# Late row blocks as three rounded products in a Fourier-filter and GEGLU kernel: splits queued behind named operations, and the first pair's place in the third tile

## The chip, the core and the metric

The kernel runs on one core of one Trainium2 chip. The metric is the device time of one execution in microseconds (us); less is better. Engines are named as in the profile: PE does matrix products (PEld is its loading of weights), ACT, DVE and POOL work element by element, and SP's queue issues the DMAs.

## What is computed

The reference is a two-part layer on a sequence of 2048 rows with 512 features. The first part is a filter in the frequency domain with a residual, the second a gated feed-forward layer with a residual:

```python
x = A_x                                           # (1, 2048, 512)
X = rfft2(layernorm(x)); X = X * (w_r + 1j * w_i)
h = x + irfft2(X)
g = layernorm(h) @ w_gate; u = layernorm(h) @ w_up     # 512 -> 1376
h2 = h + (gelu(g) * u) @ w_down                        # 1376 -> 512
```

All inputs and outputs are fp32.

## The kernel before, in words

The rows are kept as 16 blocks of 128 (`NB` = 16); `gh[:, b]` in SBUF is block b, 128 partitions by 512 features. The filter is done as dense products with tables. Its last step for a block is the inverse transform over rows, one product of the 128x128 table `mis[:, b]` with the block's unfolded spectrum `gh[:, b]`, then a DVE operation that adds x, subtracts the mean and writes h back into `gh[:, b]`, and DVE statistics for the second layernorm.

The feed-forward layer works on half of the blocks at a time (q = 0: blocks 0 to 7, q = 1: blocks 8 to 15), and within a half on 11 tiles of 128 hidden units; 22 tiles in all, counted by n. A tile is seven groups of products, P0 to P6 (a Strassen-like scheme), each of six matmuls of 128x128 by 128x512, since each fp32 product is made from three rounded ones: a value is split into a rounded high part (ACT, type fp32r) and a low part (what is left, by a subtraction on DVE or POOL), and high by high, high by low and low by high are added up (`mm3`, L96 to L103; its three matmuls are at L100, L101 and L102).

`gate_up(n)` (L694) is a generator that records a tile in seven steps: P0 and copy c1; P1 and the addition d1; P2 and c2; P3; P4, c3 and dy; P5 with the first half's gelu, product m0 and split i0, o0; P6 with d2 and the second half's m1, i1, o1. The copies are at L651 (ACT), the additions d1, d2, dy at L654 (DVE), gelu at L657 (ACT), m at L660 (DVE), i at L666 (ACT, high part), o at L673 (DVE, low part). The products go to banks 0 to 2 of PSUM for even n, 3 to 5 for odd n. `down` (L732) records the products with w_down (L747) of a group of two or three finished tiles, one block of rows at a time, into bank 6 or 7 in turn (`bank_67`), each followed by a DVE addition into `gh` (L753, or L750 with the output's DMA). `fill(2)` records two such blocks.

Weights for a later tile come by `load_gu` (L127): two DMAs, four POOL operations (L138 to L146), one rounding copy of 128x1792 on DVE (L153, CAST), and three POOL subtractions for the low parts (L156: one of 128x256, two of 128x768). The rounded copy goes to one of two buffers, so it waits for the products of the tile two before. The helper `behind` (L116) gives as the reason of one such wait that it "leaves the shared port" to a DVE instruction. w_down comes by `load_d` (L489: a DMA, ACT L494, POOL L496).

While the first half's tiles run, the second half's blocks are finished off beside them: blocks 8, 12 and 9 were unfolded already, the others are unfolded by four POOL operations of 128x256 each (L809 to L812) when `late(b)` (L946) is first advanced; the second advance records the DMA of x (L954), the product (L956, one fp32 matmul, which the profile shows as two MATMUL records), the residual (L957, DVE) and the statistics (L505, L507). Blocks 8 and 12 have their products in tile 2, blocks 9 and 13 in tile 3, 10 in tile 4, 14 in tile 5, 11 in tile 6, 15 in tile 7. The py of such a block lies in bank 6 or 7, in the same turn as the `down` blocks.

What sets the order: up to the start of tile 2 a list written by hand (`FIRST`) fixes the order of PE, ACT, DVE and POOL. In the loop from n = 2 (L978) only PE's order is as recorded; a scheduler that simulates the engines places ACT's, DVE's and POOL's instructions when it builds the program, and each engine then runs its instructions in that fixed order, each waiting for its semaphores. `tc.issue_after(i)` keeps an instruction behind i in that placing. `reuse_waits` and the buffer counts of the pools (`w3`: two buffers unless said otherwise) set when a buffer comes free.

In the loop, one turn n advances the tile n: P1, then P2, then the second advance of the waiting `late` blocks, `fill(2)`, P3, `fill(2)`, P4, `fill(2)`, P0 of the tile n+1, `fill(2)`, the first advance of the next `late` blocks, P5, P6.

Of the kernel before, what the change touches and what calls it, by code (L numbers as in the profile page):

```python
# [12 lines left out]
F32 = mybir.dt.float32  # L13
F32R = mybir.dt.float32r
I32 = mybir.dt.int32
AF = mybir.ActivationFunctionType
ALU = mybir.AluOpType
PSUM = bass.MemoryType.PSUM

S, D, F = 2048, 512, 1376  # L20
P = 128
# [36 lines left out]
def kernel(  # L58
# [15 lines left out]
    nc = tc.nc  # L74
    pe, act, dve, pool = nc.tensor, nc.scalar, nc.vector, nc.gpsimd
# [423 lines left out]
    def row():  # L499
        return rp.tile([P, D], F32, name="row")  # L500
# [141 lines left out]
    def tile_of(n, i=slice(0, 4)):  # L642

        at = slice(i.start * P, i.stop * P)
        (x, y, z), by_pe = products(n, i)
        if n not in sums:
            sums[n] = sum_tiles()
        s1, u2, u3 = (t[:, at] for t in sums[n])

        def copy(to, a):  # L650
            return lambda: act.activation(to, a, AF.Copy)  # L651

        def add(to, a, b):
            return lambda: dve.tensor_tensor(to, a, b, op=ALU.add)  # L654

        def gelu(g):
            return lambda: act.activation(g, g, AF.Gelu_apprx_tanh)  # L657

        def times(u, g):
            return lambda: dve.tensor_tensor(u, u, g, op=ALU.mult)  # L660

        def high(k, u):
            def do():
                if n not in parts_of:
                    parts_of[n] = w3.tile([P, 2, 2, 512], F32R, name="a", bufs=3)
                act.activation(parts_of[n][:, 0, k, at], u, AF.Copy)  # L666

            return do

        def low(k, u):  # L670
            def do():
                a = parts_of[n][:, :, k, at]
                dve.tensor_tensor(a[:, 1], u, a[:, 0].bitcast(F32), op=ALU.subtract)  # L673

            return do

        return by_pe | {
            "c1": copy(s1, x),
            "d1": add(s1, y, s1),
            "c2": copy(u2, x),  # L680
            "c3": copy(u3, x),
            "dy": add(y, z, u3),
            "G0": gelu(s1),
            "m0": times(x, s1),
            "i0": high(0, x),
            "o0": low(0, x),
            "d2": add(u2, z, u2),
            "G1": gelu(u2),
            "m1": times(y, u2),
            "i1": high(1, y),  # L690
            "o1": low(1, y),
        }

    def gate_up(n):  # L694

        do = products(n)[1] if n == 2 else tile_of(n)

        def all_of(names):
            for k in names.split():
                ins = do[k]()  # L700
            return ins

        all_of("P0")
        if n == 2:

            yield
            do = tile_of(n)
            all_of("c1 P1 d1")
        else:
            all_of("c1")  # L710
            yield
            all_of("P1 d1")
        yield
        for names in ("P2 c2", "P3"):
            all_of(names)
            yield
        last = copied[n] = all_of("P4 c3")
        all_of("dy")
        yield

        for _ in load_d(tiles[n][1], last):
            pass

        for names in ("P5", "P6 d2"):
            all_of(names)
            k = names[1] == "6"
            with tc.issue_after(last.ins):
                do[f"G{k:d}"]()
            all_of(f"m{k:d} i{k:d} o{k:d}")
            yield  # L730
# [38 lines left out]
    orders = [list(range(NF)), [NF - 2, NF - 1, *range(NF - 3, -1, -1)]]  # L769
    tiles = [(q, f) for q, order in enumerate(orders) for f in order]  # L770
    downs = iter(())
    begun_tiles, wds, parts_of, hns, copied, sums = {}, {}, {}, {}, {}, {}
    bank_67 = itertools.cycle((6, 7))

    def sum_tiles():
# [11 lines left out]
    do = {}  # L787
# [140 lines left out]
    def step(n):  # L928

        if n not in begun_tiles:  # L930
            f = tiles[n][1]
            if f not in gu:
                for _ in load_gu(f):
                    pass
            begun_tiles[n] = gate_up(n)
        next(begun_tiles[n])
# [3 lines left out]
    with tc.manual_schedule(engines={et.PE, et.Activation, et.DVE, et.Pool}):  # L940
        for op in FIRST.split():
            name, *place = op.split(".")
            do[name](*map(int, place))


    def late(b):  # L946

        if b not in BY_THEN:

            with held("lo"):  # L950
                unfolded(b, row())
        yield
        xt = row()
        nc.sync.dma_start(xt, x3[:, b])  # L954
        py = ps[:, next(bank_67)]
        pe.matmul(py, mis[:, b], gh[:, b], start=True, stop=True)  # L956
        dve.scalar_tensor_tensor(gh[:, b], xt, mv[:, b, 0:1], py, op0=ALU.subtract, op1=ALU.add)  # L957
        for _ in stats2(b):
            pass
        yield  # L960
# [7 lines left out]
    def fill(n):  # L968
        for _ in range(n):
            next(downs, None)  # L970
# [7 lines left out]
    with tc.manual_schedule(engines={et.PE}):  # L978
        for n, (q, f) in list(enumerate(tiles))[2:]:
            k, at_change = n - q * NF, n == NF - 1  # L980
            if k == 0:
                step(n)
            step(n)
            if k > 8 and not q:
                for i in range(2 * k - 18, 2 * k - 16):
                    with tc.issue_after(copied[n - 1].ins):
                        hns[i] = [normed(b) for b in (8 + i, 12 + i)]
            step(n)
            if at_change:

                steps = [in_turn(i, hns[i], banks) for i, banks in enumerate(((3, 4), (5, 0), (3, 4), (1, 2)))]
                next(steps[0])
            for g in ending:
                next(g)
            if n in (6, 7):

                norm_scales(2 * n - 4, 2)
            fill(2)
            step(n)
            fill(2)  # L1000
            step(n)
            fill(2)

            if k == NF - 1:
                downs = down(q, orders[q][-3:], True)
            if at_change:
                next(steps[0])
                next(steps[1])
            elif k < NF - 1:
                step(n + 1)  # L1010
                fill(2)
            else:
                fill(1)
            ending = [late(b) for b in lates.get(n, ())]
            for g in ending:
                next(g)
            step(n)
            step(n)
            if k in (4, 7):
                downs = down(q, orders[q][: k + 1][-3:], False)  # L1020
            elif k == 1:
                downs = down(q, orders[q][:2], False)
            if at_change:
                gu = {f: gu[f] for f in orders[0][-2:]}
                for s in steps:
                    for _ in s:
                        pass
                    fill(2)
            if k == NF - 1:
                fill(12)  # L1030
# [125 lines left out]
```

## Time and profile before

| what | value |
| --- | --- |
| time, median of 3 runs | 455.23 us (455.15 to 455.26) |
| the profiled execution's own time | 455.09 us |
| its span (first to last instruction) | 453.3 us |
| PE busy / PEld / DVE / ACT / POOL | 438.1 / 371.2 / 276.7 / 206.5 / 276.0 us |
| granted PE clock, mean over the span | 0.998 |
| DMA moved | 41.05 MB, mean 91 GB/s |
| part of the span this change touches (tile 2's P2 to tile 7's late product) | 131.8 to 214 us |

In the rows of the trace's timeline the columns are: start and length in us, engine, line of the kernel, operation, the tiles it writes and reads, shapes, count, and in brackets the idle time before it with what ended it. Successive instructions of one engine overlap by some 0.04 to 0.17 us in these records, so the distance from start to start is the cost of one in a dense row. A row with a count of 2 or more covers several instructions merged. In the groups by line, the numbers after the bar are the busy time in us and the mean ns of one.

### The profile page before, as it was taken

Reading aid. Unit: us, or ns where it says so; the run is one execution under the profiler, and the core shown is the slowest. Engines: PE = TensorE matmul, PEld = TensorE weight load, DVE = VectorE, ACT = ScalarE, POOL = GpSimd, SP = SyncE. Lnnn points to the kernel's source line nnn. Section 1 sums busy time; section 2 is a strip of 40 time slices with the busy share of each in tenths; the row PEclk is TensorE's granted clock in tenths of the full one; section 3 lists DMA queues with packets and bytes.
Section 4 is the critical chain, followed back from the end, with each engine's and each line's share of the span. In section 5 each row is a group of like instructions: output and inputs, shape, how many; then the busy total and the mean of one; then the engine's idle time right before and its main releaser. Section 6 shows DMA issues by size and latency. Waiting matters only on the chain.

```text
span 453.3 us, 6435 instructions
## 1 busy us (share of the span) xinstructions
PE 438.1 (97%) x2289; PEld 371.2 (82%) x2289; DVE 276.7 (61%) x513; ACT 206.5 (46%) x433; POOL 276.0 (61%) x305
## 2 busy tenths in 40 slices
PE   3999999999999999999999999999999999999996
PEld 3999998788878777877888888888888888888875
DVE  5957886797565766358734579266655355635453
ACT  4979776688741243034322775242243024303420
POOL 6985996968869578738662643165566546663210
PEclk9999999999999999999999999999999999999999
DMA  8994805200032022112210213121122102210013
GB/s 293 392 395 145 274 11 185 95 25 1 25 116 74 31 83 93 48 46 71 69 46 25 70 40 123 48 93 46 26 69 71 46 24 71 69 46 25 23 70 117
DMA packets 21168, 41.05 MB, mean 91 GB/s; under 512 B 2064, under 2 KB 7696, under 8 KB 21008
## 3 DMA queue, kind: packets, MB, share of 16 engines
q1 hardware_dynamic: 20992, 40.51, 25.9%
q8 instruction: 18, 0.29, 0.3%
q10 hardware_dynamic: 144, 0.13, 0.1%
q14 instruction: 14, 0.11, 0.1%
HBM read 36.44 MB, written 4.19 MB: 90 GB/s over the span
## 4 chain that ended last, share of the span: by engine, by line
PE 93%; DVE 3%; ACT 2%; DMA 1%; issue 1%; SPq 0%; DVEq 0%
PE ps L747 26%; PE ps L100 15%; PE ps L102 15%; PE ps L101 15%; PE ps L288 5%; PE ps L416 3%; PE ps L515 3%; PE ps L427 3%; PE ps L448 2%; PE ps L848 1%; PE ps L956 1%; DMA gh<-in_x 1%; PE ps L554 1%; PE ps L548 1%; PE ps L845 0%
## 5 line engine op out<-in xcount | busy, mean ns | idle before, releaser
L100 PE MATMUL ps<-cb,gu 128*128 128x512 f32 (+1 forms) x336 | 127.8, 380 | 2.0 <-ACT s L651 1.6
L747 PE MATMUL ps<-wd,a 128*128 128x512 f32 (+1 forms) x537 | 125.9, 387 | 0.2 <-DVE gh L750 0.2
L102 PE MATMUL ps<-cb,gu 128*128 128x512 f32 (+1 forms) x336 | 124.8, 372 | 0.0
L101 PE MATMUL ps<-cb,gu 128*128 128x512 f32 (+1 forms) x336 | 124.8, 371 | 0.0
L747 PEld LDWEIGHTS ps<-wd,a 128*128 128x128 f32 x537 | 99.3, 188 | 22.0 <-DVE gh L957 1.0
L156 POOL TENSOR_TENSOR gu<-raw,gu 128x768 fp32r<-128x768 f32 (+1 forms) x54 | 78.3, 1479 | 39.8 <-DVE gu L153 36.0
L651 ACT ACTIVATE s<-ps 128x512 f32<-128x512 f32 (+1 forms) x72 | 40.4, 561 | 133.7 <-PE ps L102 133.4
L100 PEld LDWEIGHTS ps<-cb,gu 128*128 128x128 f32 x336 | 63.2, 188 | 14.9 <-ACT s L651 2.2
L101 PEld LDWEIGHTS ps<-cb,gu 128*128 128x128 f32 x336 | 63.3, 188 | 11.7 <-issue 1.0
L102 PEld LDWEIGHTS ps<-cb,gu 128*128 128x128 f32 x336 | 63.2, 188 | 11.0
L753 DVE TENSOR_TENSOR gh<-ps,gh 128x512 f32<-128x512 f32 x48 | 33.1, 691 | 53.4 <-PE ps L747 53.3
L496 POOL TENSOR_TENSOR wd<-wdr,wd 128x512 fp32r<-128x512 f32 x22 | 28.5, 1295 | 50.9 <-ACT wd L494 50.9
L660 DVE TENSOR_TENSOR ps<-ps,s 128x512 f32<-128x512 f32 (+1 forms) x48 | 31.0, 650 | 24.8 <-PE ps L102 22.5
L666 ACT ACTIVATE a<-ps 128x512 fp32r<-128x512 f32 (+1 forms) x48 | 26.9, 561 | 38.9 <-DVE ps L660 38.6
L138 POOL TENSOR_TENSOR raw<-raw 128x256 f32<-128x256 f32 x20 | 14.7, 737 | 38.3 <-DMA raw<-in_wgu 37.2
L673 DVE TENSOR_TENSOR a<-ps,a 128x512 fp32r<-128x512 f32 (+1 forms) x48 | 30.8, 641 | 11.5 <-ACT a L666 9.8
L654 DVE TENSOR_TENSOR s<-ps,s 128x512 f32<-128x512 f32 (+1 forms) x48 | 30.9, 643 | 10.3 <-PE ps L102 8.7
L657 ACT ACTIVATE s<-s 128x512 f32<-128x512 f32 (+1 forms) x48 | 28.2, 592 | 18.4 <-DVE s L654 18.4
L654 DVE TENSOR_TENSOR ps<-ps,s 128x512 f32<-128x512 f32 (+1 forms) x24 | 15.7, 654 | 27.7 <-ACT s L651 27.7
L288 PE MATMUL ps<-ms,pn 128*128 128x128 f32 x120 | 17.4, 295 | 7.6 <-ACT ms L256 7.4
L288 PEld LDWEIGHTS ps<-ms,pn 128*128 128x128 f32 x120 | 16.0, 209 | 8.0 <-POOL pn L263 7.4
L153 DVE CAST gu<-raw 128x1792 fp32r<-128x1792 f32 x18 | 19.6, 1091 | 4.5 <-PE ps L101 2.9
(124 smaller groups left out, 609.6 us busy)
## 6 DMA issues: line engine op xcount, KB each, us to landing
raw<-in_wgu SPq DMA_DIRECT2D x40, 256.0 KB, 3.1
wt<-in_w SPq DMA_DIRECT2D x16, 520.0 KB, 5.5
wdr<-in_wd SPq DMA_DIRECT2D x22, 256.0 KB, 2.7
out<-gh SPq DMA_DIRECT2D x15, 256.0 KB, 2.0
gh<-in_x SPq DMA_DIRECT2D x7, 512.0 KB, 8.0
row<-in_x SPq DMA_DIRECT2D x12, 256.0 KB, 3.0
mis<-in_mi SPq DMA_DIRECT2D x1, 1024.0 KB, 10.8
a<-in_x SPq DMA_DIRECT2D x4, 256.0 KB, 4.1
```

The source lines that it names most:

```text
L100: pe.matmul(o, lh, rh, start=(i == 0 and not onto), stop=False, skip_group_check=True)
L101: pe.matmul(o, lh, rl, start=False, stop=False, skip_group_check=True)
L102: last = pe.matmul(o, ll, rh, start=False, stop=(i == n - 1), skip_group_check=True)
L156: pooled["lo"] = pool.tensor_tensor(r[:, 1, m], t[:, m], r[:, 0, m].bitcast(F32), op=ALU.subtract)
L288: pe.matmul(pt[:, c], o, mc, start=(z == 0), stop=(z == len(parts[b][c]) - 1))
L496: pool.tensor_tensor(r[:, 1], t, r[:, 0].bitcast(F32), op=ALU.subtract)
L651: return lambda: act.activation(to, a, AF.Copy)
L654: return lambda: dve.tensor_tensor(to, a, b, op=ALU.add)
L660: return lambda: dve.tensor_tensor(u, u, g, op=ALU.mult)
L673: dve.tensor_tensor(a[:, 1], u, a[:, 0].bitcast(F32), op=ALU.subtract)
L747: pe.matmul(o, parts_of[tiles.index((q, f))][:, ha, i // 4, r], wds[f][:, hw, c], start=start, stop=stop)
L753: dve.tensor_tensor(gh[:, b, c], o, gh[:, b, c], op=ALU.add)
```

## The change

The single fp32 product of a late block becomes three rounded ones (`mm3`), for which both factors are split: two ACT copies (high parts of `gh[:, b]`, 128x512, and of `mis[:, b]`, 128x128) and two DVE subtractions (low parts), all from SBUF to SBUF. `late` gets a third stage: first advance unfolds, second splits, third does the product. The splits are kept behind two given operations: in tile 2 behind the last high and low part of the hand-written list (g1bi1, g1bo1), from tile 3 on behind the tile's c1 (ACT) and d1 (DVE). From tile 3 on the product stays behind P2; for the pair of tile 2 (blocks 8 and 12) it moves behind P4, past two `fill(2)`. The scratch for DMA descriptors is set to 4096 bytes, and two tiles `m` and `v` of two buffers each are new.

```diff
 def high(k, u):
-                act.activation(parts_of[n][:, 0, k, at], u, AF.Copy)
+                return act.activation(parts_of[n][:, 0, k, at], u, AF.Copy)
 def low(k, u):
-                dve.tensor_tensor(a[:, 1], u, a[:, 0].bitcast(F32), op=ALU.subtract)
+                return dve.tensor_tensor(a[:, 1], u, a[:, 0].bitcast(F32), op=ALU.subtract)
...
             do = tile_of(n)
-            all_of("c1 P1 d1")
+            begun[n] = do["c1"](), (do["P1"](), do["d1"]())[1]
         else:
-            all_of("c1")
+            c1 = do["c1"]()
             yield
-            all_of("P1 d1")
+            begun[n] = c1, (do["P1"](), do["d1"]())[1]
...
-            do[name](*map(int, place))
+            ins = do[name](*map(int, place))
+            if name == "g1bi1":
+                behind_act = ins
+            elif name == "g1bo1":
+                behind_dve = ins
...
     def late(b):
...
+        yield
+        m = w3.tile([P, 2, P], F32R, name="m")
+        v = w3.tile([P, 2, D], F32R, name="v")
+        for h, l, full in ((v[:, 0], v[:, 1], gh[:, b]), (m[:, 0], m[:, 1], mis[:, b])):
+            with tc.issue_after(behind_act.ins):
+                act.activation(h, full, AF.Copy)
+            with tc.issue_after(behind_dve.ins):
+                dve.tensor_tensor(l, full, h.bitcast(F32), op=ALU.subtract)
         yield
         xt = row()
         nc.sync.dma_start(xt, x3[:, b])
         py = ps[:, next(bank_67)]
-        pe.matmul(py, mis[:, b], gh[:, b], start=True, stop=True)
+        mm3(py, [((m[:, 0], m[:, 1]), (v[:, 0], v[:, 1]))])
...
             step(n)
+            if n > 2:
+                behind_act, behind_dve = begun[n]
+            for g in ending:
+                next(g)
...
             step(n)
-            for g in ending:
-                next(g)
+            if n > 2:
+                for g in ending:
+                    next(g)
...
             fill(2)
             step(n)
             fill(2)
             step(n)
+            if n == 2:
+                for g in ending:
+                    next(g)
             fill(2)
...
-    nc = bacc.Bacc("TRN2", target_bir_lowering=False, num_devices=1)
+    nc = bacc.Bacc("TRN2", target_bir_lowering=False, num_devices=1, dynamic_dma_scratch_size=4096)
```

In the diff of the loop, the four `step(n)` shown are P1, P2, P3 and P4 of the turn. `begun[n]` holds c1 and d1 of tile n.

In the built programs the change shows as follows. On DVE the new subtractions stand directly behind d1 of tiles 3 to 7, in the order v, m (v, m, v, m in tile 3), and m1 (L660), the residual (now L969) and o1 (L673) of the tile come behind them. In tiles 3 and 6 DVE's order ahead of them is CAST, d2, o0, d1, as before; in tile 4 the CAST moves from behind m1 to ahead of d1; in tiles 5 and 7 it stays behind m1. In tile 2 they stand behind the last o of the hand-written list, mixed with the first two `down` additions and ahead of the CAST. ACT's new copies stand behind c1, ahead of i0 or i1. On POOL one w_down subtraction (L496) moves ahead of two unfolding operations in tile 2. SP's order is the same.

More of the change, by code (lines that the diff above doesn't have):

```diff
@@ L771 @@
     downs = iter(())
-    begun_tiles, wds, parts_of, hns, copied, sums = {}, {}, {}, {}, {}, {}
+    begun_tiles, wds, parts_of, hns, copied, sums, begun = {}, {}, {}, {}, {}, {}, {}
     bank_67 = itertools.cycle((6, 7))
```

## The prediction

> **What bounds the kernel now.** I read the page first: busy time by engine, then the chain of work that ended last. Both say PE.
>
> ```profile
> PE 438.1 (97%) x2289; PEld 371.2 (82%) x2289; DVE 276.7 (61%) x513; ACT 206.5 (46%) x433; POOL 276.0 (61%) x305
> ...
> PE 93%; DVE 3%; ACT 2%; DMA 1%; issue 1%; SPq 0%; DVEq 0%
> ```
>
> Then the stage itself, by windows (length first, then busy time of PE, PEld, DVE, ACT and POOL):
>
> ```profile
> 131.77:142.01 10.24, 10.19 (x41) 7.35 (x40) 6.54 (x11) 0.60 (x1) 8.36 (x9) 1.00 0.14 47
> 154.26:165.54 11.28, 11.28 (x47) 8.64 (x46) 8.15 (x15) 4.53 (x8) 9.84 (x11) 1.00 0.29 93
> 213.14:453.30 240.16, 236.46 (x1064) 195.54 (x1062) 128.79 (x205) 84.25 (x156) 112.57 (x107) 1.00 0.17 57
> ```
>
> PE has no gap in the stage, and almost none in the 240 us behind it (236.46 of 240.16). So whatever PE loses or gains here arrives at the end in full, and PE only loses if something makes it wait. POOL works 9.84 of 11.28 us in the tile of the second row; that matters below.
>
> **The products.** PE's timeline, tile 3: 24 rounded products, then two fp32 products in four records.
>
> ```profile
> 148.81 0.39 PE L100 MATMUL ps<-cb,gu 128*128 128x512 f32 x1
> ...
> 154.03 0.39 PE L102 MATMUL ps<-cb,gu 128*128 128x512 f32 x1
> 154.26 1.88 PE L956 MATMUL ps<-gh,mis 128*128 128x512 f32 x4
> ```
>
> From 148.81 to 154.03 are 23 steps, 0.227 us each. The fp32 records end at 156.14 and the last rounded one at 154.42, so four records cost 1.72, or 0.86 a product. Three rounded ones cost 0.68. The gain is 0.18 a block, 1.4 us for eight blocks, if PE never waits. That is the whole prize, 0.3%.
>
> **What is added and can make PE wait.** Per block, two copies on ACT and two subtractions on DVE. ACT is idle where they stand, for instance 4.22 us ahead of i0 in tile 2's end:
>
> ```profile
> 151.18 0.60 ACT L666 ACTIVATE a<-ps 128x512 fp32r<-128x512 f32 x1 [4.22 <-DVE ps L660]
> ```
>
> Four copies of at most that row's 0.60 fit, so the high parts cost nothing. The subtractions are another matter: both inputs lie in SBUF, unlike the sums of the tiles, which read one from PSUM. The trace has few such DVE instructions; here are two places.
>
> ```profile
> 14.39 1.55 DVE L277 TENSOR_TENSOR uv<-pn 128x512 f32<-128x512 f32 x1
> 14.12 1.27 POOL L263 TENSOR_TENSOR pn<-gh 128x512 f32<-128x512 f32 x1
> 15.35 1.73 POOL L262 TENSOR_TENSOR pn<-gh 128x512 f32<-128x512 f32 x1
> 28.62 0.42 DVE L275 TENSOR_TENSOR us<-pn 128x256 f32<-128x256 f32 x1
> 73.04 1.87 POOL L94 TENSOR_TENSOR gu<-raw,gu 128x256 fp32r<-128x256 f32 x2
> 73.31 1.01 DVE L438 TENSOR_TENSOR z<-t,t 128x520 f32<-128x520 f32 x1
> 74.36 0.57 DVE L440 TENSOR_TENSOR z<-z 128x2 f32<-128x2 f32 x1
> ```
>
> L277 starts at 14.39 while POOL's L263 runs to 15.39, and ends at 15.94: it waited out the POOL instruction and then took 0.55. POOL's next one started at 15.35 and took 1.73 for 1.27: it waited meanwhile. The two exclude each other. The last three rows tell who is next when both want to go: POOL's second L94 stood waiting while L438 ran to 74.32; the tiny L440 came 0.04 later, and still took until 74.93, past the end of the L94 pair (74.91). So they alternate, one instruction each. With no POOL instruction in the way I take 0.60 from start to start for v (the step of the rows below) and 0.2 for m, estimated from 0.42 for 256 columns less 0.13 for each 128 (0.60 for 512 against 0.34 for 256); behind POOL 0.55 and 0.16.
>
> The Trainium skill (SBUF — State Buffer, Who interferes with whom) says the same: a DVE instruction with two SBUF inputs contends with a GpSimd instruction that reads SBUF, the loser being held for the whole instruction. By that rule the sum is the one below; without it, it is that of the third rival. The rows agree with it (1.55 for 0.55 at work).
>
> **Tile 3.** Call E the start of its P1 (151.53). P2 ends at E+2.73, and then PE wants v9's low part at E+2.96 (second product) and m9's at E+3.19.
>
> ```profile
> 151.56 1.09 DVE L153 CAST gu<-raw 128x1792 fp32r<-128x1792 f32 x1 [0.42 <-PE ps L101]
> 152.57 0.68 DVE L654 TENSOR_TENSOR s<-ps,s 128x512 f32<-128x512 f32 x1
> 153.17 0.68 DVE L673 TENSOR_TENSOR a<-ps,a 128x512 fp32r<-128x512 f32 x1
> 153.77 0.68 DVE L654 TENSOR_TENSOR s<-ps,s 128x512 f32<-128x512 f32 x1
> ...
> 152.74 4.34 POOL L156 TENSOR_TENSOR gu<-raw,gu 128x256 fp32r<-128x256 f32 x3 [4.48 <-DVE gu L153]
> 157.03 0.76 POOL L809 TENSOR_TENSOR row<-gh 128x256 f32<-128x256 f32 x1
> ...
> L156 POOL TENSOR_TENSOR gu<-raw,gu 128x768 fp32r<-128x768 f32 x36 | 65.8, 1849 | 0.0
> ```
>
> DVE is behind already: CAST, d2, o0, and d1 only at E+2.24. The subtractions stand behind d1, so v9 comes at E+2.84, where POOL is in the second of the three L156, which runs to E+3.75. Then, in turn: v9 to 4.30, third L156 to 6.10 (1.85 less the overlap of starts), m9 to 6.26, L809 (0.72 a step) to 6.98, v13 to 7.53, L810 to 8.25, m13 to 8.41. PE does what it can between; the last product waits for m13. A restart costs 0.17, by the rows of tile 2 below. End at 8.41 + 0.17 + 0.23 = E+8.81, before E+2.73+1.72 = E+4.45. **Tile 3: +4.4.** Behind these on DVE wait m1, the residuals and o1; they take some 2.5 us, to about E+11; PE asks for them at P1 of tile 4 (o1's bank), five groups of six (6.8 us) after E+8.8, so they cost nothing.
>
> **Tiles 4 and 6.** In tile 4 the CAST moves ahead of d1:
>
> ```profile
> 162.82 0.39 PE L100 MATMUL ps<-cb,gu 128*128 128x512 f32 x1
> 163.63 0.68 DVE L673 TENSOR_TENSOR a<-ps,a 128x512 fp32r<-128x512 f32 x1
> 165.59 1.08 DVE L153 CAST gu<-raw 128x1792 fp32r<-128x1792 f32 x1
> 166.75 2.54 POOL L156 TENSOR_TENSOR gu<-raw,gu 128x256 fp32r<-128x256 f32 x2 [1.57 <-DVE gu L153]
> ...
> 200.02 1.09 DVE L153 CAST gu<-raw 128x1792 fp32r<-128x1792 f32 x1 [0.42 <-PE ps L101]
> 201.20 4.35 POOL L156 TENSOR_TENSOR gu<-raw,gu 128x256 fp32r<-128x256 f32 x3 [3.03 <-DVE gu L153]
> ```
>
> With E = 162.82, o0 is at E+0.81, so CAST E+1.42, d1 E+2.43, v10 E+3.03. L156 follows the CAST's start by 1.16: E+2.6, its short one to E+3.3. v10 to 3.87, long L156 to 5.70, m10 to 5.86, end E+6.26; before E+2.73+0.86 = E+3.59. **+2.7.** Tile 6 has tile 3's order (E = 199.99, CAST E+0.03, L156 E+1.21): m11 to E+6.26, end E+6.66. **+3.1.** The CAST of tile 4 also waits for POOL's chain; PE's delay in tile 3 gives that chain more time than the subtractions take from it, so I add nothing.
>
> **Tiles 5 and 7.** The CAST stays behind, and d1 comes at E+1.57 (E = 173.24), v at E+2.17:
>
> ```profile
> 174.81 0.69 DVE L654 TENSOR_TENSOR s<-ps,s 128x512 f32<-128x512 f32 x1
> 177.57 0.74 POOL L146 TENSOR_TENSOR raw<-raw 128x256 f32<-128x256 f32 x1
> ```
>
> Free of POOL, both are in time: gain 0.18. POOL's chain that ends with this L146 (E+5.1) comes some 3 us earlier against E, since PE is late, so one instruction may still be met: -0.2 to +0.9, I take **+0.5 for tile 5 and -0.2 for tile 7** (two tiles' delay ahead of it).
>
> **Tile 2.**
>
> ```profile
> 131.77 1.88 PE L956 MATMUL ps<-gh,mis 128*128 128x512 f32 x4
> 133.69 3.02 PE L747 MATMUL ps<-wd,a 128*128 128x512 f32 x12
> 136.55 0.39 PE L100 MATMUL ps<-cb,gu 128*128 128x512 f32 x1
> ...
> 137.91 2.90 PE L747 MATMUL ps<-wd,a 128*128 128x512 f32 x12
> 140.65 0.39 PE L100 MATMUL ps<-cb,gu 128*128 128x512 f32 x1
> ...
> 132.89 0.75 DVE L957 SCALAR_TENSOR_TENSOR gh<-row,mv,ps 128x512 f32<-128x512 f32 x1 [1.27 <-issue]
> 132.21 0.73 POOL L138 TENSOR_TENSOR raw<-raw 128x256 f32<-128x256 f32 x1 [3.61 <-DMA raw<-in_wgu]
> ```
>
> Before, twelve L747 waited for the residual to free bank 6: it ended at 133.64, they began at 133.69 and took 2.86 for 2.74; so a restart costs 0.05 + 0.12. The pair and these twelve took 4.78. Behind P4 the pair meets the same wait: three products end sooner (0.68), the residual starts 0.26 later (132.89 against 131.77 + 0.86) and takes 0.75, so twelve begin at +1.75 for 1.36 of products, a wait of 0.5 for 0.33 before. The pair itself gains 0.36. Net -0.2. Against it: the subtractions come in turn with POOL's L138 to L146 (0.74 each): L138 to 132.94, v8 133.5, L142 134.2, m8 134.4, L144 135.1, v12 135.6, and only then the first `down` addition, which frees bank 6 at 136.2. The second `fill` wants that bank at 131.77 + 2.74 + 1.36 = 135.9, so PE waits 0.3 and restarts: +0.5. **Tile 2: +0.3.** SP's order is unchanged, and the DMAs of x are issued where they were; the smaller scratch touches no instruction in the order.
>
> **Sum.** 0.3 + 4.4 + 2.7 + 0.5 + 3.1 - 0.2 = +10.8 on the profiled 455.09 (0.14 under the median of the runs, which I leave aside): 465.9, say **466.0**. Its own range is 463 to 468, from a meeting with one POOL instruction more or less.
>
> **Rivals.**
> - *DVE goes twice.* If a DVE instruction right behind another keeps its turn, only v waits. Tile 3: v9 4.30, m9 4.45, v13 5.0, end E+5.6, +1.2; tile 4 +0.9; tile 6: m11 4.45, end E+4.93, +1.3; tiles 2, 5, 7 together -0.1. Sum +3.3: 458.4. For it: L440 had to wait for L438's result, so it wasn't right behind. Against: the POOL instruction has waited longer.
> - *No exclusion for these shapes.* Tile 3: v9 E+3.5, m9 3.7, v13 4.3, m13 4.5, end E+4.85, +0.4; tile 4 +0.7, tile 6 +0.6; the others -0.2 each, sum +1.2: 456.3. Against: L277's 1.55.
> - *Faster: the low parts come in time.* One mechanism: d1 and the subtractions done before PE's second late product in every tile, v by E+2.96; then only the products count, -1.4: 453.7. The point where it turns is d1's start: E+1.6 or earlier wins 0.18 a block, E+2.24 (tiles 3 and 6) can't, since v9's start alone is E+2.84 and takes 0.6. It needs DVE to be ahead of its own order of before; nothing in the change takes work off it.
>
> **Chances.** Forecast 0.62, DVE twice 0.18, no exclusion 0.10, low parts in time 0.05, a sum between these within 0.9 us of before 0.05. The range must take in the first two: 457.5 to 468. What can be told from no change is 0.2%, 0.9 us: faster 0.05, within 0.05, slower 0.90.
>
> **What would show it.** Right: in tiles 3, 4 and 6 of the changed profile PE stands idle in front of the late block's L101 and L102, ended by DVE m and v (L963); L963 rows of 128x512 of 1 to 2 us with a POOL row ending inside them, 128x128 rows of 1 to 2 us, and POOL's L156 of 2.4 us there. In tile 7 no wait. DVE twice: short 128x128 rows. No exclusion: 0.7 and 0.3 us throughout. Wrong altogether: no idle PE in front of L101 and L102.

## The result and the profile after

| | before | after |
| --- | --- | --- |
| median | 455.25 us (455.06 to 456.76, 6 runs) | 468.24 us (467.06 to 471.65, 6 runs) |
| profiled execution, its span | 455.09, 453.3 us | 468.48, 466.7 us |
| granted PE clock over the span | 0.998 | 0.989 |

The changed kernel takes 1.029 times as long (95% interval 1.027 to 1.031). Forecast was 466.0 us and a range of 457.5 to 468.0: the sign and the places hold, and the time lies 0.24 us above the upper end. Its runs spread with the granted clock: 467.06 us at a mean of 0.993, 471.65 at 0.981; a later run (the last experiment) took 465.71 at 0.996.

First the page's line of busy time. PE's busy time has grown by 5.7 us although its products have become fewer microseconds of work, so something ran slower; the line of the granted clock, in 40 slices of 11.7 us, shows a 7 (152 to 163 us) and an 8 (175 to 187 us), where before (the last line) had nines.

```profile
PE 443.8 (95%) x2297; PEld 375.5 (80%) x2297; DVE 291.7 (63%) x529; ACT 212.5 (46%) x449; POOL 279.0 (60%) x305
...
PEclk9999999999999798999999999999999999999999
...
PEclk9999999999999999999999999999999999999999
```

Next, what PE waited for between 130 and 230 us (total, times, longest). Apart from one wait of 0.2 us of `down`, these are the two operands that the prediction named, and nothing else.

```profile
PE ps L102 <- DVE m L963: 4.2, 4, 1.3
PE ps L101 <- DVE v L963: 3.4, 4, 1.2
```

The stage by windows, each from one start of P1 to the next (the first from the end of tile 2's P2; columns as in the prediction, the clock is the first number behind ACT's and POOL's).

```profile
131.79:151.29 19.50, 19.34 (x85) 15.70 (x84) 12.47 (x21) 5.88 (x14) 15.32 (x16) 1.00 0.21 75
151.29:168.93 17.64, 14.91 (x49) 10.73 (x48) 13.29 (x18) 5.26 (x11) 11.42 (x11) 0.81 0.10 33
168.93:183.39 14.46, 12.34 (x46) 9.52 (x45) 9.61 (x13) 4.75 (x10) 9.73 (x11) 0.88 0.23 74
...
210.61:223.97 13.36, 10.81 (x46) 8.37 (x45) 11.70 (x24) 5.27 (x11) 10.26 (x10) 1.00 0.21 69
```

Set against before's stretches (its starts are 131.77, 151.53, 162.82, 173.24, 199.99, 210.41 and the end 453.3):

| stretch | before | after | difference | forecast |
| --- | --- | --- | --- | --- |
| tile 2 | 19.76 | 19.50 | -0.26 | +0.3 |
| tile 3 | 11.29 | 17.64 | +6.35 | +4.4 |
| tile 4 | 10.42 | 14.46 | +4.04 | +2.7 |
| tile 5 and the `down` run behind it | 26.75 | 27.22 | +0.47 | +0.5 |
| tile 6 | 10.42 | 13.36 | +2.94 | +3.1 |
| tile 7 to the end | 242.89 | 242.73 | -0.16 | -0.2 |
| sum | | | +13.4 | +10.8 |

Three of the six agree within 0.2 us. Tile 2 is 0.6 us better than forecast, and tiles 3 and 4, which are 2.0 and 1.3 us worse, are those whose clock column reads 0.81 and 0.88. PE's timeline of tile 3 parts the two effects: first the waits, then slow rows.

```profile
154.01 0.39 PE L100 MATMUL ps<-v,m 128*128 128x512 f32 x1
155.62 0.49 PE L101 MATMUL ps<-v,m 128*128 128x512 f32 x1 [1.23 <-DVE v L963]
157.44 0.53 PE L102 MATMUL ps<-v,m 128*128 128x512 f32 x1 [1.32 <-DVE m L963]
157.78 0.63 PE L100 MATMUL ps<-v,m 128*128 128x512 f32 x1
...
159.34 0.79 PE L102 MATMUL ps<-v,m 128*128 128x512 f32 x1
159.93 0.63 PE L100 MATMUL ps<-cb,gu 128*128 128x512 f32 x1
...
164.62 0.39 PE L102 MATMUL ps<-cb,gu 128*128 128x512 f32 x1
```

P3 starts at 159.93, that is E+8.64 (forecast E+8.81). From there on its matmuls come at a step of 0.43 us and are 0.63 long, against 0.227 and 0.39 at full clock, and only the twelfth (164.62) is of the old length: eleven steps of 0.2 us too much, 2.2 us. That is the difference between +6.35 and the +4.2 of the waits. Windows over 158 to 164 us and, in tile 4, over 175 to 178 us give a granted clock of 0.50. In tile 4 the same:

```profile
172.84 0.50 PE L101 MATMUL ps<-v,m 128*128 128x512 f32 x1 [0.80 <-DVE v L963]
174.66 0.67 PE L102 MATMUL ps<-v,m 128*128 128x512 f32 x1 [1.32 <-DVE m L963]
175.12 0.63 PE L100 MATMUL ps<-cb,gu 128*128 128x512 f32 x1
...
178.41 0.39 PE L102 MATMUL ps<-cb,gu 128*128 128x512 f32 x1
```

P3 is at E+6.19 (forecast E+6.26), and the eight matmuls from 175.12 to 178.41 take 3.29 where eight steps of 0.227 would be 1.82: 1.4 to 1.5 us. In tile 6 the waits are those of tile 3 (1.23 and 1.32) and the clock stays at 1.00.

DVE and POOL over the same time show why v and m are late, row by row as the prediction had them:

```profile
154.13 1.45 DVE L963 TENSOR_TENSOR v<-gh,v 128x512 fp32r<-128x512 f32 x1
155.50 1.89 DVE L963 TENSOR_TENSOR m<-mis,m 128x128 fp32r<-128x128 f32 x1
157.31 1.22 DVE L963 TENSOR_TENSOR v<-gh,v 128x512 fp32r<-128x512 f32 x1
158.46 0.83 DVE L963 TENSOR_TENSOR m<-mis,m 128x128 fp32r<-128x128 f32 x1
159.21 0.69 DVE L660 TENSOR_TENSOR ps<-ps,s 128x512 f32<-128x512 f32 x1
```

```profile
152.49 4.74 POOL L156 TENSOR_TENSOR gu<-raw,gu 128x256 fp32r<-128x256 f32 x3 [3.17 <-DVE gu L153]
157.20 0.78 POOL L809 TENSOR_TENSOR row<-gh 128x256 f32<-128x256 f32 x1
157.94 1.19 POOL L810 TENSOR_TENSOR row<-gh 128x256 f32<-128x256 f32 x1
```

The last of the three L156 ends at 157.23, and m9, which had stood since 155.50, ends 0.16 later, at 157.39: a row of 1.89 us for what takes 0.28 at its shortest (157.23 is 152.49 + 4.74). L809 ends at 157.98, v13 0.55 later, and L810 in turn waits for v13 (1.19 for 0.74). L660, with one input in PSUM, is back at 0.69.

### The profile page after: what moved, and what is told of

The parts are those of the page before. It is cut to its first block, busy times and chain, and to the rows that moved or that the text cites. A ratio compares the mean times of both kernels' runs of the same rounds, so it can differ in the third digit from the quotient of the medians.

```text
span 466.7 us, 6480 instructions
## 1 busy us (share of the span) xinstructions
PE 443.8 (95%) x2297; PEld 375.5 (80%) x2297; DVE 291.7 (63%) x529; ACT 212.5 (46%) x449; POOL 279.0 (60%) x305
## 4 chain that ended last, share of the span: by engine, by line
PE 87%; DVE 7%; ACT 2%; issue 1%; DMA 1%; DVEq 0%
PE ps L747 25%; PE ps L102 15%; PE ps L100 15%; PE ps L101 14%; PE ps L288 4%; PE ps L416 3%; PE ps L515 3%; PE ps L427 3%; PE ps L448 2%; DVE m L963 1%; DVE v L963 1%; PE ps L848 1%; PE ps L554 1%; DMA gh<-in_x 1%; DVE s L654 1%
## 5 line engine op out<-in xcount | busy, mean ns | idle before, releaser
L101 PE MATMUL ps<-cb,gu 128*128 128x512 f32 (+1 forms) x336 | 126.4, 376 | 0.0
L102 PE MATMUL ps<-cb,gu 128*128 128x512 f32 (+1 forms) x336 | 126.2, 375 | 0.0
L747 PE MATMUL ps<-wd,a 128*128 128x512 f32 (+1 forms) x537 | 125.5, 387 | 0.3 <-DVE gh L750 0.2
L747 PEld LDWEIGHTS ps<-wd,a 128*128 128x128 f32 x537 | 99.4, 188 | 21.2 <-DVE gh L750 0.6
L156 POOL TENSOR_TENSOR gu<-raw,gu 128x768 fp32r<-128x768 f32 (+1 forms) x54 | 79.6, 1501 | 40.1 <-DVE gu L153 38.9
L651 ACT ACTIVATE s<-ps 128x512 f32<-128x512 f32 (+1 forms) x72 | 40.4, 561 | 133.7 <-PE ps L102 133.4
L100 PEld LDWEIGHTS ps<-cb,gu 128*128 128x128 f32 x336 | 64.2, 191 | 14.2 <-ACT s L651 2.2
L101 PEld LDWEIGHTS ps<-cb,gu 128*128 128x128 f32 x336 | 64.3, 191 | 11.3
L102 PEld LDWEIGHTS ps<-cb,gu 128*128 128x128 f32 x336 | 64.2, 191 | 11.4
L753 DVE TENSOR_TENSOR gh<-ps,gh 128x512 f32<-128x512 f32 x48 | 33.1, 690 | 51.5 <-PE ps L747 51.3
L496 POOL TENSOR_TENSOR wd<-wdr,wd 128x512 fp32r<-128x512 f32 x22 | 28.4, 1290 | 61.3 <-ACT wd L494 61.3
L660 DVE TENSOR_TENSOR ps<-ps,s 128x512 f32<-128x512 f32 (+1 forms) x48 | 31.0, 650 | 24.4 <-PE ps L102 22.2
L138 POOL TENSOR_TENSOR raw<-raw 128x256 f32<-128x256 f32 x20 | 15.2, 762 | 38.1 <-DMA raw<-in_wgu 37.0
L673 DVE TENSOR_TENSOR a<-ps,a 128x512 fp32r<-128x512 f32 (+1 forms) x48 | 30.8, 641 | 11.4 <-ACT a L666 9.8
## 6 DMA issues: line engine op xcount, KB each, us to landing
mis<-in_mi SPq DMA_DIRECT2D x1, 1024.0 KB, 10.8
```

The lines of the kernel that those rows point to most:

```text
L100: pe.matmul(o, lh, rh, start=(i == 0 and not onto), stop=False, skip_group_check=True)
L101: pe.matmul(o, lh, rl, start=False, stop=False, skip_group_check=True)
L102: last = pe.matmul(o, ll, rh, start=False, stop=(i == n - 1), skip_group_check=True)
L156: pooled["lo"] = pool.tensor_tensor(r[:, 1, m], t[:, m], r[:, 0, m].bitcast(F32), op=ALU.subtract)
L496: pool.tensor_tensor(r[:, 1], t, r[:, 0].bitcast(F32), op=ALU.subtract)
L673: return dve.tensor_tensor(a[:, 1], u, a[:, 0].bitcast(F32), op=ALU.subtract)
```

## The experiments

All times are medians; ratios are to the kernel before on the same chip (455.31, 455.69 and 455.36 us in the three groups of runs: first the four up to `e4`, then `e5` to `e8`, then `e9` to `e11`).

The recorded expectations call the waits theory A and the late DVE queue alone theory B; here A is called W.

**Theory W** (waits): DVE's subtractions and POOL's instructions exclude each other and alternate, PE waits for the low parts, and each us of wait is a us of time. **Theory C** (clock): beyond W, the waits bring PE's granted clock to half for some us, which costs the 3.6 us that W lacks. Rivals: the place of tile 2's pair or the added instructions as such cost; DVE and POOL do not exclude each other, and the subtractions are only late in DVE's queue (theory B).

### e1_pair_only: tile 2's change alone

```diff
+        if b in (8, 12):
...
+            mm3(py, [((m[:, 0], m[:, 1]), (v[:, 0], v[:, 1]))])
+        else:
+            pe.matmul(py, mis[:, b], gh[:, b], start=True, stop=True)
```

> Only blocks 8 and 12 (tile 2) keep the three rounded products, behind P4; blocks 9 to 15 go back to one fp32 product without splits. If the loss is made by tiles 3 to 6 (theory A: DVE's subtractions held by POOL there; theory B: DVE's own backlog there) this kernel is 0.2 to 0.3 us faster than the kernel before (455.0), because the changed profile reaches P1 of tile 3 at 151.29 instead of 151.53. If the rounded form itself or the longer DVE and ACT queues cost, it is slower than before by 1 us or more.

Measured: 455.17 us (454.51 to 455.76), ratio 0.999 (0.998 to 1.000). So the pair, its splits among `down`'s additions and its later place cost nothing; the loss lies from tile 3 on.

### e2_splits_unread: the splits without their readers

From tile 3 on the splits are made, but the product is the fp32 one of unsplit factors; its output is the same sum, not made from three rounded products.

```diff
-        mm3(py, [((m[:, 0], m[:, 1]), (v[:, 0], v[:, 1]))])
+        if b in (8, 12):
+            mm3(py, [((m[:, 0], m[:, 1]), (v[:, 0], v[:, 1]))])
+        else:
+            pe.matmul(py, mis[:, b], gh[:, b], start=True, stop=True)
```

> Everything of the change stays but the late products of tiles 3 to 7, which are one fp32 product of the unsplit factors again; the splits are still made, and nobody reads them. If the loss is PE's wait for the low parts (theories A and B alike), the subtractions stay as long as in the changed kernel (128x512 up to 1.4 us, 128x128 up to 1.9 us) and the time is that of before within 0.5 us (454.7 to 455.7), with the granted clock back at 0.998. If the longer DVE and POOL queues cost by themselves, it is 2 us or more above before.

Measured: 458.88 us, ratio 1.008 (1.006 to 1.010). It misses: 3.6 us are lost though no product reads a low part. PE's waits are now others, ahead of the next tile's products. First the waits (130 to 230 us), then m1 on DVE and what stands on ACT in tile 3:

```profile
PE ps L100 <- DVE ps L654: 1.3, 2, 1.0
PE ps L100 <- ACT s L651: 1.1, 1, 1.1
```

```profile
159.14 0.68 DVE L660 TENSOR_TENSOR ps<-ps,s 128x512 f32<-128x512 f32 x1
```

```profile
159.86 0.60 ACT L666 ACTIVATE a<-ps 128x512 fp32r<-128x512 f32 x1 [5.17 <-DVE ps L660]
160.35 0.59 ACT L651 ACTIVATE s<-ps 128x512 f32<-128x512 f32 x1
```

DVE is held by the four subtractions until 159.14; m1 (L660) behind them is late, so ACT idles 5.17 us ahead of the high part i1, and the copy c2 (L651), which PE's next products wait for, stands in ACT's queue behind that i1. A blocked DVE queue therefore costs by itself, through m1 and ACT's order. In the changed kernel this doesn't show, because PE is late already: the two waits lie side by side and the longer one counts. From late product to late product, the stretch from tile 3 to tile 4 takes 13.97 us (before 11.28), from tile 5 to tile 6 27.30 (26.75) and from tile 6 to tile 7 11.34 (10.42). The waits quoted are 2.4 us of it; the causes of the rest were not traced.

### e3_low_from_psum: one input of the subtraction in PSUM

From tile 3 on ACT writes a full copy to PSUM as well, and the low part is taken from that.

```diff
...
             with tc.issue_after(behind_act.ins):
                 act.activation(h, full, AF.Copy)
+                for o in by_ps:
+                    act.activation(o, full, AF.Copy)
+                    full = o
...
```

> From tile 3 on ACT copies the factor into PSUM as well, and the subtraction reads it from there, so it has one SBUF input instead of two; its place in DVE's order behind d1 stays. Theory A (it is held by POOL's instructions because both inputs lie in SBUF): 128x512 rows of 0.7 us, 128x128 rows of 0.3 us, POOL's L156 back at 1.85 us, tiles 3, 4 and 6 lose 0.3 to 0.8 us each, no fall of the clock, 455.7 to 457. Theory B (only the queue ahead of it on DVE): the same waits as in the changed kernel and 466 to 468.

Measured: 457.73 us, ratio 1.005 (1.004 to 1.006), 10.5 us under the changed kernel. The subtractions' forms (count, then ns at the least, the median and the most):

```profile
L972 DVE TENSOR_TENSOR v<-ps,v x6: 678/679/680, 153.8 to 215.0; 128x512 fp32r<-128x512 f32 x6
L972 DVE TENSOR_TENSOR m<-ps,m x6: 277/279/280, 154.4 to 215.6; 128x128 fp32r<-128x128 f32 x6
```

```profile
PE ps L100 <- DVE v L972: 1.7, 2, 0.9
```

All twelve now take the same time to within 3 ns, at the same places beside the same POOL instructions, where the changed kernel had up to 1.45 and 1.89 us. So the lengthening goes with the second input in SBUF, and the rival by which they are only late falls. The time misses the expectation by 0.7 us: the copy for v lies in the bank of the product itself, so the product's first matmul waits for the subtraction (1.7 us in two waits), a cost of the experiment, not of the change; one more wait, of 0.8 us for a copy of ACT (L651), is left.

### e4_fillers and e5_fillers_pinned: PE kept busy in its waits

Blocks 9, 10 and 11 get useless matmuls (four, then six, into a bank that a later product starts anew) ahead of the product's second and third matmul, so that PE works where it would wait. In the first kernel the scheduler then moved the CAST ahead of d1 or d2 in tiles 4, 5 and 7; the second one keeps the CASTs behind o0 of tile 3 and m1 of tiles 4 and 6, which gives DVE the changed kernel's order but for the turn of o1 and one residual.

```diff
...
+        for c, (lhs, rhs) in ((4, (h, rl)), (6, (l, r))):
+            for _ in range(c if b in (9, 10, 11) else 0):
+                pe.matmul(z, h, r, start=True, stop=True, skip_group_check=True)
+            pe.matmul(py, lhs, rhs, start=False, stop=lhs is l, skip_group_check=True)
```

> The changed kernel with useless matmuls in PE's waits: for blocks 9, 10 and 11 four more rounded products (0.91 us) ahead of the second and six (1.36 us) ahead of the third late product, written to the bank that P3 starts afresh. Theory C (the rest of the loss, some 3.6 us, is PE's granted clock falling after the waits): no MATMUL of 0.63 us behind them, clock 0.996 to 0.998, and a time of 464 to 466, that is 2.5 to 4 us faster than the changed kernel, though it does more. If the slow rows behind the waits have another cause, it is as slow as the changed kernel or slower (468 to 470).

Measured for the first: 472.21 us, ratio 1.037 (1.035 to 1.039). It misses, since its moved CASTs make new waits of 0.80 and 1.31 us in tiles 5 and 7, where no useless matmuls stand. Its time says nothing on the clock, but its trace does. The first row is P3 of tile 4, behind filled waits, the others are tile 5:

```profile
173.57 0.40 PE L100 MATMUL ps<-cb,gu 128*128 128x512 f32 x1
...
184.34 0.50 PE L974 MATMUL ps<-v,m 128*128 128x512 f32 x1 [0.80 <-DVE v L963]
186.16 0.79 PE L974 MATMUL ps<-v,m 128*128 128x512 f32 x1 [1.31 <-DVE m L963]
186.75 3.48 PE L747 MATMUL ps<-wd,a 128*128 128x512 f32 x9
```

Behind the filled waits of tiles 3, 4 and 6 every matmul has its full-clock length. Behind the empty ones the eighteen L747 of tile 5 take 5.54 us (4.24 at full clock, by `e7`), and P3 of tile 7 has seven matmuls of 0.59 to 0.63. So one run shows both sides: filled waits cost no clock, empty ones do.

> The kernel with the useless matmuls again, but with three CASTs kept behind the operations behind which the changed kernel has them (o0 of tile 3, m1 of tiles 4 and 6), since in the first try the fillers had moved CASTs ahead of d1 in tiles 5 and 7 too. DVE's order is now that of the changed kernel but for the turn of o1 and a residual. Theory C (after PE's waits its clock falls, some 3.6 us of the loss): no MATMUL of 0.63 us, clock 0.996 or more, and 464 to 466. If the clock is not what costs, 468 or more.

Measured for the second: 464.52 us (463.84 to 466.31), ratio 1.021 (1.018 to 1.023), so 3.7 us less than the changed kernel with more work on PE. The two ran in different groups: against the kernel before of its own group it is 8.8 us slower, the changed kernel 13.0. Its four runs read a granted clock of 0.998 to 1.000, the seven of the changed kernel 0.981 to 0.996. Its tiles 3 and 4 by windows:

```profile
150.91:166.15 15.24, 14.25 (x60) 10.66 (x58) 13.35 (x18) 5.27 (x11) 12.31 (x12) 1.00 0.14 40
166.15:179.06 12.91, 12.91 (x56) 10.18 (x55) 9.73 (x13) 5.26 (x11) 9.47 (x9) 1.00 0.22 77
```

The clock stays at 1.00, and the tiles take 15.24 and 12.91 us instead of 17.64 and 14.46, 4.0 us less. P3 itself starts only 0.2 and 0.1 us sooner (159.32 and 172.24, E+8.41 and E+6.09), so 3.6 of the 4.0 are matmuls at full instead of half clock. DVE is as late as before. Theory C holds.

### e6_early: the splits a tile sooner

The splits stand behind c3 and dy of the tile before, so that DVE has them done ahead of the late product.

```diff
-            begun[n] = do["c1"](), (do["P1"](), do["d1"]())[1]
+            all_of("c1 P1 d1")
...
-        all_of("dy")
+        begun[n] = last, all_of("dy")
...
             ending = [late(b) for b in lates.get(n, ())]
+            for g in ending:
+                next(g)
+            behind_act, behind_dve = begun[n]
             for g in ending:
                 next(g)
```

> The splits of blocks 9 to 15 are recorded one step of the loop earlier, behind c3 (ACT) and dy (DVE) of the tile before; the products stay where they are. Theory A and B: most low parts are there before PE wants them, though they may still meet POOL; tiles 3, 4, 6 and 7 gain 0.2 to 0.4 us each, only tile 5 still waits, some 0.7 us, because block 14 is unfolded late. 454.5 to 455.3, no fall of the clock. If three rounded products are slower in themselves, above 456.

Measured: 456.73 us (455.71 to 458.06), ratio 1.002 (1.001 to 1.003). The 13 us are nearly all back, but it is a touch slower than before, not faster. Two places are left: a wait of 1.34 us of a `down` group in tile 2 (L747), because DVE's subtractions for blocks 9 and 13 now stand ahead of its addition (L753), and 0.8 us in tile 5, because block 14 is unfolded too late:

```profile
177.64 0.49 PE L100 MATMUL ps<-v,m 128*128 128x512 f32 x1
178.37 0.50 PE L101 MATMUL ps<-v,m 128*128 128x512 f32 x1 [0.23 <-DVE v L963]
```

Unfolding (POOL's L812) ends at 176.93, and only then can the split begin; the product wants it at 177.45, where P2 ends, and is 0.8 us late when it is done.

### e7_early_spread, e9_order_alone, e10_spread_again: places for the products

On top of the earlier splits, block 14's product moves behind P4 of tile 5, and the pair of tile 2 goes one behind P3 and one behind P4. `e9` has these places with the fp32 products and without any split; `e10` is `e7` again beside it.

```diff
...
-            if n > 2:
+            if n not in (2, 5):
                 for g in ending:
                     next(g)
...
+            if n == 2:
+                next(ending[0])
             fill(2)
             step(n)
-            if n == 2:
-                for g in ending:
-                    next(g)
+            if n in (2, 5):
+                next(ending[-1])
```

> As the early splits, and block 14's product behind P4 of tile 5, and of the pair of tile 2 one behind P3 and one behind P4, so that no down block waits for a residual. By the sums of the prediction's terms every wait is gone: tile 2 gains 0.7, tile 3 0.35, the others 0.18 each, 1.7 us in all: 453.4 (453.0 to 454.2). A time of 455 or more would say that the gain is eaten elsewhere.

> The places of the kernel that spreads the products (tile 2's pair one behind P3 and one behind P4, block 14's product behind P4 of tile 5), with the late products left as fp32 ones and without any splits. It tells whether that kernel's gain comes of the three products or of the places. Theory: of the products, 0.18 us each, 1.4 us for eight; the places alone are worth what the late waits of before cost, two restarts of 0.17 at most. Expected 455.0 to 455.7, within 0.2% of before and 1.2 us or more above that kernel. Rival: the places make the gain; then 453.6 to 454.3.

> The kernel with the early splits and the spread products once more, beside the one that has its places alone, on one chip. Theory: 453.8 again (453.4 to 454.2), 0.25 to 0.4% under before, and under the places alone by 1.2 us or more, all of it eight times 0.18. Rival: the two are within 0.4 us of each other, and the three products bring nothing.

Measured: `e7` 453.84 us, ratio 0.996 (0.995 to 0.998), and again 454.06, 0.998 (0.997 to 0.999); the places alone 455.33, 0.9995 (0.9985 to 1.0005). So with next to nothing waiting, the three products win 1.3 us over the places alone, 0.16 for each of the eight blocks where the prediction took 0.18, and the places win nothing by themselves. The two intervals leave room for 0.6 to 2.0 us. This is the fastest of all kernels here. One wait of PE between 130 and 230 us is left in `e7`, 0.3 us of `down` (L747) for a residual (L969).

### e8_low_on_pool: POOL subtracts

From tile 3 on POOL makes the low parts, so that DVE and POOL never both want to go for them.

```diff
-                dve.tensor_tensor(l, full, h.bitcast(F32), op=ALU.subtract)
+                (dve if n < 3 else pool).tensor_tensor(l, full, h.bitcast(F32), op=ALU.subtract)
```

> The low parts of blocks 9 to 15 are made by POOL, at the scheduler's place, not by DVE; all else as in the changed kernel. Theory A: nothing shares the port then; POOL's rows are 1.3 us (v) and 0.4 us (m) with no lengthening of others; only tile 5 waits, some 1.5 us, because block 14's v stands behind its late unfolding. 455 to 456.5. Theory B agrees on the time but says nothing on POOL's rows. If POOL becomes the bound, above 458.

Measured: 460.57 us, ratio 1.010 (1.008 to 1.012): 4 us or more over the expectation. Tiles 3, 4 and 6 have no wait for a low part; the loss is nearly all in tile 5 (0.4 us more is a wait for a CAST, at 221 us). PE in tile 5:

```profile
177.76 0.51 PE L100 MATMUL ps<-v,m 128*128 128x512 f32 x1 [2.06 <-ACT v L961]
179.13 0.50 PE L101 MATMUL ps<-v,m 128*128 128x512 f32 x1 [0.87 <-POOL v L963]
...
179.70 5.89 PE L747 MATMUL ps<-wd,a 128*128 128x512 f32 x18
```

POOL's queue, longer by its own subtractions, ends block 14's unfolding (L812) at 177.04; ACT's high part must follow and PE waits 2.06, then 0.87 for POOL's low part (its 128x512 takes 1.30, DVE's 0.68). And the clock term again: the eighteen L747 behind these waits take 5.89 us, where `e7` has 4.24. The waits and this 1.65 make 4.6 of the 5 us. The four runs, on one chip, follow the clock: 459.56 us at 0.996, 460.18 at 0.995, 460.96 and 461.11 at 0.991. POOL's rows were not all free of lengthening either: in tile 3 DVE's CAST, which has one input, took 1.77 us for 1.09 while POOL's first v ran, and POOL's next m took 1.31 for 0.46. So POOL seems able to hold not only DVE's instructions with two inputs in SBUF; this is one case, not tested further.

### e11_changed_again: the changed kernel, another profile

> The changed kernel once more with a profile of its own. Theory: the waits for the low parts come again in tiles 3, 4 and 6 at the same places and within 0.2 us of the same lengths, since the order and the alternation set them, while the stretches at half the granted clock need not fall in the same tiles. So the start of P3 after the start of P1 is again E+8.6 (tile 3), E+6.2 (tile 4), E+6.5 (tile 6), within 0.2, and what differs between the two profiled spans is the number of matmuls at a step of 0.427 us, 0.2 us each. Rival: the slow stretches belong to the places (tiles 3 and 4 always, tile 6 never), as an effect of what stands there.

Measured: 465.71 us, span 463.9. PE in tiles 3 and 4, then the windows of these two tiles:

```profile
156.10 0.49 PE L101 MATMUL ps<-v,m 128*128 128x512 f32 x1 [1.23 <-DVE v L963]
157.92 0.65 PE L102 MATMUL ps<-v,m 128*128 128x512 f32 x1 [1.32 <-DVE m L963]
...
160.40 0.63 PE L100 MATMUL ps<-cb,gu 128*128 128x512 f32 x1
...
173.48 0.50 PE L102 MATMUL ps<-v,m 128*128 128x512 f32 x1 [1.31 <-DVE m L963]
173.82 0.39 PE L100 MATMUL ps<-cb,gu 128*128 128x512 f32 x1
```

```profile
151.76:167.76 16.00, 13.38 (x50) 9.64 (x48) 13.29 (x18) 5.28 (x11) 11.42 (x11) 0.89 0.12 37
167.76:180.66 12.90, 10.79 (x47) 8.36 (x45) 9.62 (x13) 4.75 (x10) 9.75 (x11) 1.00 0.24 84
```

The waits are the same to 0.01 us (1.23, 1.32, 1.31), and P3 starts at E+8.64, E+6.06 and (tile 6) E+6.49. But only three matmuls of P3 in tile 3 are slow, not eleven, and none in tile 4: 3.2 us less in these two tiles. So the waits belong to the kernel, and how much clock they cost differs from run to run; this is one run of another group, but the six of the first group spread too (0.981 to 0.993), as do the four of `e8`. In tile 6 no matmul was slow in either profile; whether it can happen there stays open.

## Why the prediction was right and where it failed

**Right: what PE waits for, where, and by which order.** The waits stand in tiles 3, 4 and 6 ahead of L101 and L102, ended by v and m, as forecast, and POOL and DVE alternate, one instruction each. Of the chain in tile 3 the forecast had v9 done at E+4.30 (measured 155.58, E+4.29), m9 at E+6.26 (157.39, E+6.10), m13 at E+8.41 (159.29, E+8.00), and P3 at E+8.81 (E+8.64). Per tile the forecast is 0.1 to 0.2 us too long (here the third L156 ended at E+5.94, not E+6.10). In tile 3 the chain was 0.4 us sooner than forecast, and the product behind it, at the lowered clock, gave 0.2 of that back: in `e5`, with the clock at 1.00, the same P3 came at E+8.41. Tiles 5 and 7 came as the text had them, +0.47 and -0.16. The second profile, with a clock of 0.996, ends 0.3 us under the forecast.

The rivals fall: DVE going twice by its short 128x128 rows (1.89 instead), no exclusion by the long rows and `e3`, in time by the waits themselves. (Where the prediction says that without exclusion the sum is that of the third rival, it is the second in its list that fits, +1.2.) The last one was right in its condition, though: with the splits a tile sooner, and the products where their unfolding allows, the gain is there (`e7`).

**Failed: the sum has no term for the clock.** The prediction added waits and restarts, and took each matmul behind a wait at 0.227 us. The runs show that two waits of 0.8 to 1.3 us shortly after each other can bring the granted clock to half, for some 3.5 to 7 us. In the profiled run this is 3.6 of the 13.4 us, counted from the start of P3; `e4` and `e5` take it away by filling the waits, and `e11` shows most of it gone in a run whose waits are the same. All other terms together are 9.8, against 10.8 forecast, so without the clock the text would have been 1 us too high. The two errors are of opposite sign: that the forecast is off by only 2.2 us is in part luck.

The Trainium skill (TensorE: Matmul & The Clock Gate, Part 1: The HAM clock gate) says that the array runs at half clock after an idle window of about 3.4 us, and that this window runs freely, not from the start of a kernel. A free window would fit what differs between the two profiles; the slow stretch of tile 4 (174.66 to 178.41, 3.75 us) is little over one such window. The rule of thumb on the same page of the Trainium skill, no idle gaps over 3.4 us, does not fit here: no single gap was longer than 1.32 us, and the clock fell. That windows of 3.4 us decide it is the statement of the Trainium skill; the runs show only the lengths.

**Failed: tile 2's +0.5.** The step took POOL's L138, v8, L142, m8, L144 and v12 in turn, POOL first and each for its whole length, with bank 6 free at 136.2. DVE and POOL of the changed kernel:

```profile
132.28 0.69 DVE L963 TENSOR_TENSOR v<-gh,v 128x512 fp32r<-128x512 f32 x1 [0.64 <-ACT v L961]
132.89 0.83 DVE L963 TENSOR_TENSOR m<-mis,m 128x128 fp32r<-128x128 f32 x1
133.64 0.68 DVE L963 TENSOR_TENSOR v<-gh,v 128x512 fp32r<-128x512 f32 x1
134.24 0.68 DVE L753 TENSOR_TENSOR gh<-ps,gh 128x512 f32<-128x512 f32 x1
```

```profile
132.32 1.25 POOL L138 TENSOR_TENSOR raw<-raw 128x256 f32<-128x256 f32 x1 [3.74 <-DMA raw<-in_wgu]
133.65 1.27 POOL L142 TENSOR_TENSOR raw<-raw 128x256 f32<-128x256 f32 x1
```

v8 started 0.04 us ahead of L138, so it was POOL that stood (1.25 for 0.74); m8 then waited for L138, and v12 again came 0.01 us ahead of L142 (1.27 for 0.74). The first addition ended at 134.92 and the `fill` of 135.87 had its bank. Who is first was decided by 40 ns; the prediction gave it one way and put no bound on the other.

**Right only under its cover: "they cost nothing".** m1, the residuals and o1 behind the subtractions were booked at nothing because PE asks for them late. `e2` shows what that cover is worth: with PE on time, the same delay of DVE costs 3.6 us, at least 2.4 of them behind ACT's and DVE's delayed queues. The step was true for this kernel, and wrong as a statement on the queue.

**Right in the small: the prize.** 0.18 us a block, from the rows; `e10` against `e9` gives 1.3 us for eight.

## What to carry to other kernels

In this kernel a DVE instruction with both inputs in SBUF is priced by the POOL instruction beside it, not by its own row (1.89 us for 0.28); put it where POOL rests, or let one input come from PSUM, before giving a product to it. When operands come late to a dense PE twice in a row, price the waits and, as a further cost that may or may not come (0 to 2.2 us a tile here), the matmuls behind them at half clock; look at the clock column of the windows before adding up waits. A gain of 0.3% in products shows only when every one of them finds its operands ready: the place of the split and of the product decided here between +13 us and -1.3.

## What the runs showed of the hardware

- Two gaps of 0.8 to 1.3 us in a row, with a single matmul between them, brought PE's granted clock to half (0.50 in the windows; step 0.43 for 0.227 us) for some 3.5 or 7 us; the same gaps in another tile or another run did it for less or not at all. With useless matmuls in them (`e4`, `e5`) the clock stayed at 1.00. It also stayed there behind two waits of 1.10 and 1.00 us with six matmuls between them (`e2`) and behind a single one of 1.34 us (`e6`). Where the limit lies was not measured.
- Where a DVE subtraction with two inputs in SBUF and POOL's instructions hold each other up, they go in turn, one instruction each: 1.45 and 1.22 us for 128x512 rows of 0.68, 1.89 and 0.83 for 128x128 rows of 0.28, with POOL's L810 at 1.19 for 0.74. A CAST on DVE met the same once (`e8`, 1.77 for 1.09).
- With one input in PSUM the same subtractions vary by 3 ns at most beside the same POOL work (`e3`, 678 to 680 and 277 to 280 ns).
